# Gated mix of memory attention and a spectral filter: interleaved q/k scratch, gate weights by matmul, stores on GpSimd's queue

## The chip, the cores and the metric

The kernel runs on one core of one Trainium2 chip. The metric is the device time of one execution in microseconds. Three executions of the kernel before took 242.58, 243.16 and 244.0 us; their median is 243.16 us. A profile was taken of one further execution.

## The reference, cut to what matters

```python
def _A_ref(x, wq, wk, wv, wo, beta):        # S=2048, D=640, H=32 heads of 20, N=4 segments of L=512
    q, k, v = (heads(x @ w) for w in (wq, wk, wv))
    g = sigmoid(beta)
    for s in range(N):                       # per head: causal softmax inside the segment
        p = softmax(qs @ ks.T * Dh**-0.5 + mask)
        a_dot = p @ vs
        a_mem = (phi(qs) @ M) / (phi(qs) @ z + 1e-6)   # phi(t) = t+1 for t > 0, else exp(t)
        o = g * a_mem + (1 - g) * a_dot
        M, z = M + phi(ks).T @ vs, z + phi(ks).sum(rows)
    return o @ wo
def _B_ref(x, w_r, w_i):                     # spectral filter over the whole 2048 x 640
    return irfft2(rfft2(x) * (w_r + 1j * w_i))
gate = sigmoid((A_x * gate_w).sum(-1))       # one gate for each row
return gate * a + (1 - gate) * _B_ref(x)     # x is A_x
```

## The kernel before, in words

**Work.** One core does both branches. Branch A goes through four segments of 512 rows. For each segment the kernel transposes x, projects q and k in five tiles of 128 features (`proj_tile`), projects v (`v_tile`), and computes causal attention for eight groups of four heads: `qk_unit` multiplies q and k, ScalarE (ACT) takes the exponential into `ex` (line 1508), the upper triangle is set to zero by `mask` on GpSimd (POOL, affine select, lines 1540 and 1549) or on VectorE (DVE, a minimum with a table, lines 1539 and 1545), and `pv_flipped` or `pv_group` multiplies with v. The memory part reads the accumulated M with phi(q) (`mem_read`) and updates it with phi(k) (`mem_update`). Branch B is a two-dimensional Fourier transform as matmuls with tables: `fold`, then the stages F1, D, T, Tb, Db and Fb. `finish_tile` adds the last stage of B and the output projection of A in one PSUM bank, and stores the rows.

**Through DRAM and back.** Heads have 20 features, tiles of a projection 128. To bring the heads to partitions 0, 32, 64 and 96, each projected tile is stored to the DRAM tensor `qk_scr` (line 582, "qk_scr<-qu", in the first segment "qk_scr<-q") and loaded again into the padded tiles `qkp` ("qkp<-qk_scr", name `pad`, four loads for each half of a segment; `pad2` in the first half of the first segment). The scratch holds, for each segment and half, a block of 320 rows of q and a block of 320 rows of k; a row is 512 tokens, 1 KB. Tile 2 of the five lies across the halves, so it is stored by two DMAs of 64 rows each:

```python
if t == 2:
    for half, p0 in ((0, 0), (1, 64)):
        self.dma(... row(half, 256 - 256 * half), [L, 64], [1, L] ..., name="st_qk")
```

The numerators of attention go through `u_scr` in the same way ("u_scr<-ub", then "oU<-u_scr"), and the memory term of segments 1 and 2 through `o_scr` ("o_scr<-mem", name `st_o`, eight stores; loaded transposed as "mT<-o_scr", line 580).

**The gate.** The weights of the gate stand as a 641st column beside each of the five tiles of `wv`, so that the second half of the v projection (321 columns) gives the gate's logits as well. They are brought there by one DMA of 640 single elements (name `ld_gw`, "wv<-in_gate_w_dram").

**Queues and order.** All DMAs are issued on SyncE's queue (SP), but for one load at the start and eight quarter stores at the end on ACT's. POOL issues none. A queue works in order: an issue that waits for its data holds up every issue behind it. The order of all work is written out: `ORDER` lists operation numbers, each with the engine that takes it, and `Sched.schedule` goes through the list, places PSUM banks, and adds waits; `ENDED` gives a ranking by which several waits of one instruction are sorted. The times in `schedule` and in the table `QUEUE` serve this planner alone. Each instruction of an engine is issued in the list's order. All matmuls are issued at lines 546 and 548, copies from PSUM at 557 (ACT) and 559 (DVE), DMAs at 582, transposing DMAs at 580.

**Where output tiles go.** `finish_tile` fills one of four tiles `ot` in two halves and stores it with one DMA of 128 rows (name `st_out`, "out_dram<-ot", twelve of them, segments 0 to 2). The last segment stores quarters (`st_part`) from SP and ACT.

Of the kernel before, what the change touches and what calls it, by code (L numbers as in the profile page):

```python
# [9 lines left out]
BF = dt.bfloat16  # L10
F32 = dt.float32

P = 128
S = 2048
D = 640
H = 32
DH = 20
NSEG = 4
L = 512
# [25 lines left out]
class Op:  # L45
    __slots__ = ("id", "alts", "preds", "succs", "prio", "banks", "nbytes", "npred", "eng", "t0", "t1",
                 "stamp", "rank", "need_inc", "dyn", "first", "outside", "name", "dma", "key", "xfer", "lock", "mode", "emode", "hold", "width", "high", "follow")


class Sched:  # L50
# [9 lines left out]
    def op(self, alts, r=(), w=(), prio=0.0, nbytes=0, name="", after=(), dma=False, xfer=0.0, lock=False, mode=0, hold=False, width=16):  # L60
# [4 lines left out]
        o.high, o.follow = False, None  # L65
# [47 lines left out]
    def schedule(self, pools, order, ended, nsem=56):  # L113
# [42 lines left out]
        sems = [[0.0, i, None] for i in range(nsem)]  # L156
        issued = []
        self.order = []
# [49 lines left out]
        while len(self.order) < len(order):  # L208
# [19 lines left out]
            if e == "pe" and o.emode != mode:  # L228
                occ += self.COST[mode, o.emode]
                mode = o.emode  # L230
            free[e] = o.t1 = t + occ
            if e == "dve" and o.lock:
                port = t + occ
            if o.dma:
                if o.hold:
                    free[e] = max(free[e], max(ring) + 170.0)
                for q in range(o.width):
                    ring[q] = max(ring[q], free[e] + 1300.0) + o.xfer
# [6 lines left out]
                sems.sort(key=lambda q: (q[0], q[1]))  # L245
                sm = sems[0]
# [13 lines left out]
        self.nsem = nsem  # L260
# [208 lines left out]
def dap(ap, off, *dims):  # L469
    return bass.AP(tensor=ap.tensor, offset=ap.offset + off, ap=[list(q) for q in dims])  # L470
# [25 lines left out]
class Kern:  # L496
# [35 lines left out]
    def mms(self, items, r, w, prio, name="", extra=0.0, mode=0):  # L532
# [17 lines left out]
        op = self.Sc.op({"pe": (f, cost, 141.0)}, r=r, w=w, prio=prio, name=name, mode=mode)  # L550
        return op
# [24 lines left out]
    def dma(self, dst, src, nbytes, r, w, prio, tr=False, name="", after=(), queue="sp"):  # L576
        def f(e):
# [3 lines left out]
            with self.nc.allow_non_contiguous_dma(reason="small strided loads"):  # L581
                return e.dma_start(d_, s_)  # L582
        cost, work, width = self.QUEUE[name] if name in self.QUEUE else self.QUEUE[name, nbytes]
        queues = ("sp", "act") if name in self.EARLY else (queue,)
        return self.Sc.op({e: (f, cost, 0.0) for e in queues}, r=r, w=w, prio=prio, nbytes=nbytes, name=name, after=after,
                          dma=True, xfer=work, hold=tr and nbytes > 500000, width=width)

    EARLY = ("ld_wqa", "ld_wka", "ld_id")
    QUEUE = {
        "ld_W": (620.0, 450.0, 16), "dup_W": (480.0, 1900.0, 16), "ld_beta": (400.0, 120.0, 16), "ld_big": (500.0, 2900.0, 16), "ld_den": (520.0, 150.0, 16),  # L590
        "ld_fcat": (400.0, 350.0, 16), "ld_g": (400.0, 1500.0, 16), "ld_gc": (580.0, 200.0, 16), "ld_gw": (420.0, 600.0, 16),
        "ld_hm": (600.0, 850.0, 16), "ld_id": (400.0, 250.0, 16), "ld_x0": (450.0, 950.0, 16), "ld_tt": (530.0, 1650.0, 16), "ld_u": (500.0, 450.0, 16),
        "ld_wka": (520.0, 1100.0, 16), "ld_wkb": (450.0, 2200.0, 16), "ld_wqa": (500.0, 1100.0, 16), "ld_wqb": (500.0, 2200.0, 16),
        "ld_wo": (600.0, 700.0, 16), "ld_wo2": (600.0, 3000.0, 16), "ld_wv": (450.0, 3000.0, 16), "ld_x": (450.0, 950.0, 16),
        "oT": (1300.0, 750.0, 16), "pad2": (370.0, 350.0, 10), "pad": (400.0, 1250.0, 10), ("pkT", 131072): (1260.0, 600.0, 16), ("pkT", 262144): (1280.0, 1100.0, 16),
        ("st_qk", 65536): (450.0, 220.0, 16), ("st_qk", 131072): (480.0, 350.0, 16), ("st_qk", 262144): (480.0, 720.0, 16), "st_g": (430.0, 150.0, 4), "st_o": (660.0, 950.0, 8), "st_out": (560.0, 1900.0, 4),
        "st_part": (430.0, 250.0, 16), "st_u": (520.0, 700.0, 16), ("xT", 131072): (1240.0, 1300.0, 16), ("xT", 262144): (1700.0, 2300.0, 16),
        ("xT", 393216): (1400.0, 2600.0, 16), ("xT", 655360): (2950.0, 2100.0, 16)}
# [1276 lines left out]
```

## Time and profile before

| | |
|---|---|
| median of three executions | 243.16 us |
| the profiled execution | 242.17 us |
| its span, first to last instruction | 240.4 us |
| matmuls | 4361 |
| bytes moved by DMA | 43.46 MB in 58072 packets, 181 GB/s in the mean |
| DMAs issued by SP and by ACT | queues q1 (42.46 MB) and q10 (0.36 MB) |

The profile shows one execution. An engine's busy time is the time in which at least one of its instructions ran; PE is TensorE's matmuls and PEld its weight loads, which overlap. A row of the windows view gives, for one stretch of time, each engine's busy time and its number of instructions in brackets, then the clock granted to TensorE (1.00 is full), the busy share of the DMA engines, and GB/s. A row of the waits view says which engine and line waited, for what, and then the total in microseconds, the number of times, and the longest. A row of a tile's view gives the shortest, median and longest duration of one instruction in nanoseconds. The chain of waits goes back from the last instruction to what released it, step by step; "SPq" is SP issuing a DMA.

### The profile page before, as it was taken

Reading aid. Unit: us, or ns where it says so; the run is one execution under the profiler, and the core shown is the slowest. Engines: PE = TensorE matmul, PEld = TensorE weight load, DVE = VectorE, ACT = ScalarE, POOL = GpSimd, SP = SyncE. Lnnn points to the kernel's source line nnn. Section 1 sums busy time; section 2 is a strip of 40 time slices with the busy share of each in tenths; the row PEclk is TensorE's granted clock in tenths of the full one; section 3 lists DMA queues with packets and bytes.
Section 4 is the critical chain, followed back from the end, with each engine's and each line's share of the span. In section 5 each row is a group of like instructions: output and inputs, shape, how many; then the busy total and the mean of one; then the engine's idle time right before and its main releaser. Section 6 shows DMA issues by size and latency. Waiting matters only on the chain.

```text
span 240.4 us, 10161 instructions
## 1 busy us (share of the span) xinstructions
PE 228.9 (95%) x4361; PEld 146.3 (61%) x4361; DVE 203.8 (85%) x493; ACT 202.7 (84%) x253; POOL 92.9 (39%) x172
## 2 busy tenths in 40 slices
PE   7999799999999999999989999999999999999993
PEld 4666367666556674654656555565555667667883
DVE  0978888999999899999999999899999679747742
ACT  2398979999999999999999999899899977678630
POOL 5203415503655407250516733504546232272810
PEclk9999999999999999999999999999999999999999
DMA  7998988678979989849986748378759862782213
GB/s 195 373 182 264 198 270 176 148 239 211 213 146 241 221 215 226 200 136 154 216 246 162 229 129 223 92 197 201 197 154 223 209 151 79 105 90 92 77 43 108
DMA packets 58072, 43.46 MB, mean 181 GB/s; under 512 B 27628, under 2 KB 55724, under 8 KB 58028
## 3 DMA queue, kind: packets, MB, share of 16 engines
q1 hardware_dynamic: 57500, 42.46, 73.9%
q8 instruction: 34, 0.56, 1.0%
q10 hardware_dynamic: 528, 0.36, 0.5%
q14 instruction: 10, 0.08, 0.1%
HBM read 22.73 MB, written 12.20 MB: 145 GB/s over the span
## 4 chain that ended last, share of the span: by engine, by line
PE 60%; DVE 15%; ACT 12%; DMA 6%; SPq 3%; issue 3%; DVEq 0%
PE psum L548 53%; ACT ex L1508 9%; PE psum L546 7%; DMA hm<-tab_hmask 3%; DMA qk_scr<-qu 2%; SPq L582 2%; DMA u_scr<-ub 2%; DVE mem L1389 1%; DVE G L559 1%; DVE oU L1791 1%; DVE ub L559 1%; DVE ex L1545 1%; DVE Pt L1696 1%; ACT qu L557 1%; DVE dn L1381 1%
## 5 line engine op out<-in xcount | busy, mean ns | idle before, releaser
L1508 ACT ACTIVATE ex<-psum 128x2048 bf16<-128x2048 f32 (+4 forms) x92 | 138.6, 1507 | 12.2 <-PE psum L548 10.7
L1549 POOL TENSOR_SCALAR_AFFINE_SELECT ex<-ex 64x256 bf16<-64x256 bf16 x66 | 26.8, 427 | 64.3 <-ACT ex L1508 63.5
L1540 POOL TENSOR_SCALAR_AFFINE_SELECT ex<-ex 128x512 bf16<-128x512 bf16 x44 | 29.4, 678 | 31.7 <-DVE ex L1545 20.3
L548 PE MATMUL psum<-qkp 20*64 20x64 bf16 (+5 forms) x1024 | 31.4, 266 | 1.6 <-ACT ex L1508 0.9
L548 PE MATMUL psum<-wv,xT 128*64 128x320 bf16 (+3 forms) x240 | 26.6, 302 | 2.4 <-DMA wv<-in_A_wv_dram 1.5
L548 PE MATMUL psum<-xT,wk 128*128 128x256 bf16 (+1 forms) x280 | 28.3, 273 | 0.0
L548 PE MATMUL psum<-xT,wq 128*128 128x512 bf16 (+1 forms) x135 | 27.9, 380 | 0.0
L1696 DVE TENSOR_TENSOR Pt<-psum,Wt 128x644 bf16<-128x644 f32 x32 | 25.8, 820 | 1.4 <-PE psum L548 1.1
L548 PEld LDWEIGHTS psum<-xT,wk 128*128 128x128 bf16 (+1 forms) x280 | 20.9, 98 | 4.4 <-issue 0.4
L548 PEld LDWEIGHTS psum<-qkp 20*64 20x64 bf16 (+1 forms) x1024 | 12.1, 100 | 18.1 <-ACT ex L1508 10.9
L546 PE MATMUL psum<-wo,oU 128*32 128x320 bf16 x480 | 21.0, 299 | 0.0
L548 PEld LDWEIGHTS psum<-wv,xT 128*64 128x64 bf16 (+1 forms) x240 | 14.8, 105 | 9.4 <-DMA wv<-in_A_wv_dram 1.7
L559 DVE CAST ot<-psum 128x320 bf16<-128x320 f32 x20 | 9.4, 489 | 10.3 <-PE psum L546 4.5
L548 PE MATMUL psum<-ex,va 128*32 128x512 bf16 (+4 forms) x480 | 17.3, 274 | 0.1
L548 PE MATMUL psum<-big,Cp 128*128 128x321 bf16 (+1 forms) x96 | 16.7, 302 | 0.7 <-DVE rs L1587 0.3
L548 PE MATMUL psum<-tt,Pt 128*128 128x128 bf16 (+1 forms) x192 | 16.4, 221 | 0.0
L1298 ACT ACTIVATE et<-qu 128x512 bf16<-128x512 bf16 x25 | 15.6, 629 | 0.4 <-DVE phk L1311 0.4
L546 PEld LDWEIGHTS psum<-wo,oU 128*32 128x32 bf16 x480 | 12.8, 97 | 3.8 <-issue 0.6
L548 PE MATMUL psum<-big,Ac 128*32 128x160 bf16 (+2 forms) x384 | 14.4, 259 | 0.7 <-DVE mem L1385 0.5
L1545 DVE TENSOR_TENSOR ex<-ex,hm 128x512 bf16<-128x512 bf16 (+1 forms) x31 | 13.8, 453 | 1.3 <-ACT ex L1508 1.0
L548 PEld LDWEIGHTS psum<-tt,Pt 128*128 128x128 bf16 (+1 forms) x192 | 12.1, 102 | 4.4 <-issue 0.9
L548 PEld LDWEIGHTS psum<-xT,wq 128*128 128x128 bf16 (+1 forms) x135 | 9.2, 97 | 8.5 <-issue 1.8
(114 smaller groups left out, 420.6 us busy)
## 6 DMA issues: line engine op xcount, KB each, us to landing
qkp<-qk_scr SPq DMA_DIRECT2D x28, 160.0 KB
qk_scr<-qu SPq DMA_DIRECT2D x12, 256.0 KB, 3.6
tt<-tab_tt SPq DMA_DIRECT2D x8, 384.0 KB, 4.4
u_scr<-ub SPq DMA_DIRECT2D x12, 256.0 KB, 3.6
Wt<-Wt SPq DMA_DIRECT2D x8, 321.0 KB, 4.0
xsb<-in_A_x_dram SPq DMA_DIRECT2D x8, 320.0 KB, 5.4
oU<-u_scr SPq DMA_DIRECT2D x15, 128.0 KB, 3.2
out_dram<-ot SPq DMA_DIRECT2D x12, 160.0 KB
```

The source lines that it names most:

```text
L546: h = e.matmul(dst, wt, r_, start=st, stop=sp_, **{**kw, "tile_position": (0, q), "skip_group_check": True})
L548: h = e.matmul(o_, l_, r_, start=st, stop=sp_, **kw)
L557: alts["act"] = (lambda e: e.activation(dst(), src(), ACT.Copy), 65 + 0.833 * n, 110.0)
L559: alts["dve"] = (lambda e: e.tensor_copy(dst(), src()), 67 + 1.04 * n, 68.0)
L582: return e.dma_start(d_, s_)
L1298: self.one("act", lambda e: e.activation(et.ap(0, [1, L]), qsl(), ACT.Exp), L, [qb], [b("et", pi_)], late, fix=94, name="phi_exp")
L1381: self.one("dve", lambda e: e.reciprocal(dn.ap(32, [1, 32]), dn.ap(0, [1, 32])), 32, [b("dn", i % 2, q) for q in range(2)], [rb], prio, fi ...
L1508: self.one("act", lambda e, d=d, q=q: e.activation(self.ex.ap(*d), self.ps(bank, *q), ACT.Exp, scale=SC), n, [bank], [self.exb(s, 2 * pr + ...
L1540: pick = lambda e: e.affine_select(ex(), ex(), [[0, 4], [1, P]], ALU.is_ge, 0.0, base=0, channel_multiplier=-1)
L1545: least = lambda e: e.tensor_tensor(dst(), src(), self.hm.ap(880 + 64 * t, [0, 4], [0, 2], [1, 64], np_=nd), ALU.min)
L1549: h = e.affine_select(self.ex.ap(e0 + d, [1280, 4], [1, 64], p0=hp, np_=np_), self.ex.ap(e0 + q, [1280, 4], [1, 64], p0=hp, np_=np_), [[0, ...
L1696: self.one("dve", lambda e, x=x, Pt=Pt, Wt=Wt, wo_=wo_, bank=bank: e.tensor_tensor(Pt.ap(x * 644, [322, 2], [161, 2], [1, 161]), self.ps(b ...
```

## The change

- **Scratch.** `qk_scr` holds, for each segment and each of the 640 features, the row of q and behind it the row of k. A load into `qkp` finds q and k of a feature side by side and moves runs of 2 KB. In `qkp` the four blocks of q and the four of k alternate, and `qk_unit` and `proj_direct` address them so. The first half of the first segment (`pad2`) keeps runs of 1 KB.
- **Middle tile.** Tile 2 is stored by one DMA of 128 rows.
- **Gate weights.** They are loaded as five rows of 128 into the tile `dnc`, turned by a matmul with the identity (`gwT`, five columns), and copied from PSUM into the column of `wv` (`ev_gw`), after `wv` has been loaded.
- **Queues.** The stores `st_out` and `st_o` are issued on POOL's queue. Fifteen names (`SPARE`) may be issued by SP or POOL, as the order says.
- **Planner.** Costs of DMAs are set anew, a DMA on POOL has a semaphore of its own, the rule that ties neighbours on POOL (`follow`) now skips DMAs, and the planner counts PE's instructions in pieces of 256. None of this is an instruction on the chip by itself; it sets waits, banks and places.
- **Order.** `ORDER` and `ENDED` are new lists. By the new list POOL issues 39 DMAs: 12 `st_out`, 8 `st_o`, 7 `ld_W`, 3 `ld_g`, 2 `dup_W`, 2 `st_g`, and one each of `ld_x`, `ld_beta`, `ld_big`, `ld_tt`, `ld_den`. SP issues 192 in place of 241. POOL has 120 operations beside its DMAs in place of 135, DVE 498 in place of 493, ACT 274 in place of 261 with its DMAs (the loads `ld_wqa` and `ld_wka` are now among them).

```diff
-        for p, o in zip(queue["pool"], queue["pool"][1:]):
-            if p.high != o.high:
-                o.follow = p
+        own = [o for o in queue["pool"] if not o.dma]
+        for p, o in zip(own, own[1:]):
+            if p.high != o.high:
+                o.follow = p
...
+            if e == "pe":
+                c = 2.011 * o.count * (4 if o.mode < 0 and o.emode == 2 else 1)
+                while stream + c > 192 + 256 * len(pieces):
+                    x = t + occ * (192 + 256 * len(pieces) - stream) / c
+                    if pieces and x < pieces[-1]:
+                        occ += pieces[-1] - x
+                        x = pieces[-1]
+                    pieces.append(x + (3000.0, 2000.0, 1000.0)[min(len(pieces), 2)] + 2550.0)
+                stream += c
...
-        queues = ("sp", "act") if name in self.EARLY else (queue,)
+        queues = ("sp", "act") if name in self.EARLY else ("sp", "pool") if name in self.SPARE else ("pool",) if name in ("st_out", "st_o") else (queue,)
...
+    SPARE = ("ld_W", "dup_W", "ld_tt", "ld_gw", "ld_beta", "ld_hm", "ld_big", "ld_wv", "ld_x", "ld_wo", "ld_wo2", "ld_g", "ld_gc", "ld_den", "st_g")
...
-        self.qkd = nc.dram_tensor("qk_scr", (NSEG, 2, 2, 320, L), BF)
+        self.qkd = nc.dram_tensor("qk_scr", (NSEG, 640, 2, L), BF)
...
-        self.dma(lambda: self.wv.ap(D, [D + 1, 5], [1, 1]), lambda: dap(self.gw_d, 0, [1, P], [P, 5], [1, 1]),
-                 P * 5 * 64, [], [self.b("gw")], 0.31, name="ld_gw")
+        self.dma(lambda: self.dnc.ap(0, [1, P], np_=5), lambda: dap(self.gw_d, 0, [P, 5], [1, P]), 5 * 256, [], [self.b("dnc")], 0.31, name="ld_gw")
+        bank = Bank(1, "gen")
+        self.mms([(lambda: (self.ps(bank, 0, [1, 5]), self.dnc.ap(0, [1, P], np_=5), self.fcat.ap(P, [1, 5], np_=5), True, True, {"tile_position": (0, 0)}), 5)],
+                 [self.b("dnc"), self.b("id"), bank], [], 0.5, name="gwT", mode=1)
+        self.Sc.op(self.copy_alts(lambda: self.wv.ap(D, [D + 1, 5], [1, 1]), lambda: self.ps(bank, 0, [1, 5], [1, 1]), 5), r=[bank, self.b("wv")], w=[self.b("gw")], prio=0.5, name="ev_gw")
...
-                self.dma(lambda j=j, pad=pad: pad.ap(0, [L, 8], [1, L], p0=32 * j, np_=DH),
-                         lambda j=j, half=half: dap(self.qkd.ap(), ((2 * s + half) * 640 + 20 * j) * L, [L, DH], [80 * L, 8], [1, L]),
+                self.dma(lambda j=j, pad=pad: pad.ap(0, [2 * L, 4], [1, 2 * L], p0=32 * j, np_=DH),
+                         lambda j=j, half=half: dap(self.qkd.ap(), ((2 * s + half) * 640 + 40 * j) * L, [2 * L, DH], [160 * L, 4], [1, 2 * L]),
...
-            for half, p0 in ((0, 0), (1, 64)):
-                self.dma(lambda half=half, p0=p0: dap(self.qkd.ap(), row(half, 256 - 256 * half), [L, 64], [1, L]), lambda p0=p0: qt.ap(qo, [1, L], p0=p0, np_=64),
-                         64 * L * 2, both, [b(which + "d", s, half, 1 - half)], prio, name="st_qk")
+            self.dma(lambda: dap(self.qkd.ap(), row(256), [2 * L, P], [1, L]), lambda: qt.ap(qo, [1, L]),
+                     P * L * 2, [qb], [b(which + "d", s, half, 1 - half) for half in range(2)], prio, name="st_qk")
...
-            self.dma(lambda: dap(self.qkd.ap(), row(t // 4, (t - slot) * P - 320 * (t // 4)), [L, P], [P * L, n], [1, L]), lambda: qt.ap(o, [L, n], [1, L]),
+            self.dma(lambda: dap(self.qkd.ap(), row((t - slot) * P), [2 * L, P], [2 * P * L, n], [1, L]), lambda: qt.ap(o, [L, n], [1, L]),
...
-                        return (self.ps(bank, hh * 512 + o, [1, n], p0=p0, np_=m), pad.ap((4 + gl) * L + KPOS[j] + kc, [1, m], p0=32 * hh, np_=DH),
-                                pad.ap(gl * L + q0, *([[-64, 2], [1, 64]] if q0 + n > L else [[1, n]]), p0=32 * hh, np_=DH), True, True, {"tile_position": (32 * hh, p0)})
+                        return (self.ps(bank, hh * 512 + o, [1, n], p0=p0, np_=m), pad.ap((2 * gl + 1) * L + KPOS[j] + kc, [1, m], p0=32 * hh, np_=DH),
+                                pad.ap(2 * gl * L + q0, *([[-64, 2], [1, 64]] if q0 + n > L else [[1, n]]), p0=32 * hh, np_=DH), True, True, {"tile_position": (32 * hh, p0)})
```

More of the change, by code (lines that the diff above doesn't have):

```diff
@@ L46 @@
     __slots__ = ("id", "alts", "preds", "succs", "prio", "banks", "nbytes", "npred", "eng", "t0", "t1",
-                 "stamp", "rank", "need_inc", "dyn", "first", "outside", "name", "dma", "key", "xfer", "lock", "mode", "emode", "hold", "width", "high", "follow")
+                 "stamp", "rank", "need_inc", "dyn", "first", "outside", "name", "dma", "key", "xfer", "lock", "mode", "emode", "hold", "width", "high", "follow", "count")
 class Sched:
@@ L64, in op @@
         o = Op()
-        o.high, o.follow = False, None
+        o.high, o.follow, o.count = False, None, 0
         o.id = len(self.ops)
@@ L550, in mms @@
         op = self.Sc.op({"pe": (f, cost, 141.0)}, r=r, w=w, prio=prio, name=name, mode=mode)
+        op.count = len(items)
         return op
@@ L588 @@
+        return self.Sc.op({e: (f, max(cost, 600.0) + 50.0 if e == "pool" else cost, 300.0 + 900.0 * (e == "pool") + 700.0 * tr) for e in queues}, r=r, w=w, prio=prio, nbytes=nbytes, name=name, after=after,
+                          dma=True, xfer=work, hold=(tr and nbytes > 500000) + 2 * tr, width=width)
+    SPARE = ("ld_W", "dup_W", "ld_tt", "ld_gw", "ld_beta", "ld_hm", "ld_big", "ld_wv", "ld_x", "ld_wo", "ld_wo2", "ld_g", "ld_gc", "ld_den", "st_g")
     EARLY = ("ld_wqa", "ld_wka", "ld_id")
@@ L1182, in proj_direct @@
         b = self.b
-        w, p0_ = (self.wq, 0) if which == "q" else (self.wk, 4 * L)
+        w, p0_ = (self.wq, 0) if which == "q" else (self.wk, L)
         pad = self.qkp[0]
```

41 lines of the change are left out of this document (23 added, 18 removed), and 500 rows, old and new, of tables (ENDED, ORDER).

## The prediction

> **What bounds the kernel now.** The profiled execution took 242.17 us: a span of 240.4 and 1.77 around it. I read the page's busy time first, then the windows of 12 us, and then who waited for whom.
>
> ```profile
> PE 228.9 (95%) x4361; PEld 146.3 (61%) x4361; DVE 203.8 (85%) x493; ACT 202.7 (84%) x253; POOL 92.9 (39%) x172
> PE 60%; DVE 15%; ACT 12%; DMA 6%; SPq 3%; issue 3%; DVEq 0%
> ```
>
> PE is busy for all but 11.5 us, and 60% of the chain is PE. The change takes away no matmul, so those 11.5 us are nearly all there is to win. Where they lie:
>
> ```profile
> 0.00:12.00 12.00, 10.68 (x164) 6.51 (x164) 6.32 (x14) 3.73 (x6) 4.88 (x13) 1.00 0.89 283
> 24.00:36.00 12.00, 10.15 (x123) 6.17 (x122) 9.75 (x26) 10.16 (x22) 3.54 (x5) 1.00 0.94 233
> 60.00:72.00 12.00, 11.57 (x250) 6.57 (x243) 11.81 (x34) 11.85 (x15) 7.30 (x18) 1.00 0.93 181
> 120.00:132.00 12.00, 11.19 (x232) 7.08 (x224) 11.87 (x29) 11.43 (x11) 4.87 (x10) 1.00 0.77 205
> 144.00:156.00 12.00, 11.37 (x205) 6.75 (x195) 10.67 (x22) 10.70 (x13) 5.09 (x11) 1.00 0.57 158
> 168.00:180.00 12.00, 11.06 (x188) 6.30 (x189) 11.86 (x30) 10.87 (x14) 5.91 (x11) 1.00 0.62 172
> 192.00:204.00 12.00, 11.29 (x307) 8.14 (x307) 10.61 (x29) 8.98 (x11) 3.12 (x6) 1.00 0.58 119
> 216.00:228.00 12.00, 12.00 (x393) 9.46 (x384) 9.49 (x23) 9.04 (x13) 7.00 (x12) 1.00 0.26 81
> 228.00:240.00 12.00, 8.83 (x244) 7.75 (x240) 4.62 (x11) 2.48 (x5) 0.80 (x1) 1.00 0.27 79
> ```
>
> The first numbers after the comma are PE, PEld, DVE, ACT and POOL; the last three are clock, DMA share and GB/s. PE stands idle 1.3 us before its first operand and 3.2 in the last stretch, after its last matmuls, which the change leaves as they are. One gap of 1.85 lies in 24 to 36; five more, of 0.4 to 0.9 each, make 3.3 between 60 and 204. So some 5 us in the middle are open to the change. In 60 to 72 DVE and ACT are as full as PE; POOL alone has room. The clock is full, so nothing is lost there.
>
> ```profile
> PE psum L548 <- DMA wv<-in_A_wv_dram: 1.5, 1, 1.5
> PE psum L548 <- DVE qu L559: 0.6, 1, 0.6
> DVE qu L559 <- DMA qk_scr<-qu: 0.9, 1, 0.9
> DVE ot L559 <- DMA out_dram<-ot: 2.0, 2, 1.1
> PEld psum L548 <- issue: 15.5, 67, 0.7
> PEld psum L548 <- POOL ex L1540: 0.9, 3, 0.4
> ```
>
> Each row is the total, the times and the longest wait. Only two of PE's waits lead to a DMA: for wv at 28 us, and for a projection buffer that its store still held at 152. The small waits are for evacuations, and these the order sets.
>
> **Part 1: gate weights.**
>
> ```profile
> 8.82 0.38 SPq L582 DMA_DIRECT2D wv<-in_gate_w_dram  x1
> 9.24 6.38 SPq L580 DMA_TRANSPOSE xT<-in_A_x_dram  x1
> 22.23 0.50 SPq L582 DMA_DIRECT2D wv<-in_A_wv_dram  x1
> wv<-in_gate_w_dram SPq DMA_DIRECT2D x1, 1.2 KB, 6.8
> wv<-in_A_wv_dram SPq DMA_DIRECT2D x1, 800.0 KB, 7.1
> ```
>
> The old load brings 640 elements one by one; it lands 6.8 us after its issue, for 1.2 KB. The new one brings five rows. It is still one SP issue, so what can be saved is time on the DMA engines, not on SP. But wv is issued at 22.23, long after the gate weights landed at 15.6, because SP was held by the transposes of x until 15.62 and then waited for a projection tile. So the gate load isn't what makes wv late. What may help is that the new order puts fewer of the eight x loads ahead of wv (one goes to GpSimd, one behind). Bounds: a gain of 1.5 (all of PE's wait) and a loss of 0.5 (two stores and a transpose of keys stand ahead of wv now). I take a gain of 0.4.
>
> ```profile
> L548 PE MATMUL psum<-fcat,omh 128*8 128x128 bf16 x8 | 1.1, 219 | 0.0
> L1340 ACT ACTIVATE gate<-psum 128x1 f32<-128x1 f32 x8 | 1.3, 165 | 0.1
> ```
>
> Added: a matmul of 5 columns and a copy of 5 columns. The nearest rows are a 219 ns matmul and a 165 ns one-column activation. The copy waits for wv and for the matmul, and the second value tile waits for the copy; behind it on ACT stand the first value evacuations. Cost 0.2, between 0 and 0.6 (if copy and hand-over all stand on PE's path).
>
> **Part 2: interleaved scratch, one store for the middle tile.**
>
> ```profile
> L582 SPq DMA_DIRECT2D qk_scr<-qu x24: 372/506/1021, 34.7 to 176.3; - x24
> L582 SPq DMA_DIRECT2D qkp<-qk_scr x36: 273/406/1148, 28.4 to 194.4; - x36
> qk_scr<-qu SPq DMA_DIRECT2D x12, 64.0 KB
> qk_scr<-q SPq DMA_DIRECT2D x4, 64.0 KB, 5.4
> 145.40 0.37 SPq L582
> 145.94 0.52 SPq L582
> 146.51 0.69 SPq L582
> 147.24 5.50 DMA qk_scr<-qu
> 152.83 0.70 DVE qu L559
> ```
>
> Sixteen half stores become eight: 8 x 0.506 = 4.0 us less of issuing on SP. The 28 large loads into qkp keep their issues, but their runs double from 1 KB to 2 KB. No row above has PE waiting for qkp by a DMA, so I give the longer runs nothing; what hides them is that these loads go out well ahead of their stage. If that cover were gone, a load would cost PE the 4.0 us median to landing. Where SP does count is the last five rows, from the chain: at 145.4 a store of u, a table copy and a store of the memory term go out ahead of the store of q or k, which takes 5.50, and the evacuation waits for its buffer. One of these four leaves SP, another may be half of a pair. PE's wait there was 0.6. With the smaller ones of its kind at 115 (a store of u) I take a gain of 0.7; bounds 0 and 1.7, about half of the 3.3 between 60 and 204.
>
> **Part 3: stores on GpSimd's queue.**
>
> ```profile
> L582 SPq DMA_DIRECT2D o_scr<-mem x8: 587/688/1337, 77.4 to 148.3; - x8
> L582 SPq DMA_DIRECT2D out_dram<-ot x20: 314/544/1255, 195.0 to 238.2; - x20
> SPq L582 <- DVE ot L559: 9.4, 2, 6.7
> POOL ex L1549 <- ACT ex L1508: 63.5, 16, 10.4
> POOL ex L1540 <- DVE ex L1545: 20.3, 7, 8.7
> 1.29 2.46 POOL L1100 MEMSET va<- 128x2832 bf16 x1
> ```
>
> SP loses 8 x 0.688 + 12 x 0.544 = 12.0 us of issues, and the wait of 9.4 in which it stood before a finished output tile while loads queued behind it. GpSimd gains 20 issues, and by the order list 19 loads that may go by either queue (tables, masks of the FFT, gates). No row shows a DMA issued by GpSimd. Below, it costs what SP pays, 0.54; above, as long as GpSimd's longest single instruction, 2.46. I take 1.0, since most of its rows lie under 1: 39 us, beside 147 idle. Each store waits for its tile (DVE, ACT), and behind it stand the causal masks of ex, for which PV on PE waits. Of POOL's idle time 63.5 + 20.3 us in 23 gaps, 3.6 each, is before just these masks, so a store of 1 us that is put into such a gap is hidden. The list also gives 15 of POOL's small operations to DVE (12 of them masks of about 0.5 us), and DVE gives about as much time in evacuations to ACT. Loss 0.3, bounds 0 and 5 (see the rivals). For SP's freedom late in the kernel: DVE waited 2.0 for output tiles, and 192 to 204 lost 0.7. Gain 0.4, bounds 0 and 0.7.
>
> [...]
>
> **Part 4: own order.** All queues are written anew. PE has the same sequence of stages; the first loads of wq and wk go from SP to ACT, which in 0 to 12 is busy for 3.7 us only, so they cost nothing there. What it can win is the rest of the 5 us in the middle, and part of PEld's 15.5 us of "issue". After 0.4, 0.7 and 0.4 some 3.5 remain; I give the order a quarter to a third of it, 0.9; bounds -3.5 and +2, since a new order opens gaps of its own (a gap here is 0.3 to 0.9, and three or four more would be 2).
>
> **Sum.** -0.4 + 0.2 - 0.7 + 0.3 - 0.4 - 0.9 = -1.9 on 242.17, so 240.3 for an execution like the profiled one. The median shown is 0.99 above it: 243.16 - 1.9 = 241.3.
>
> **The rivals.** *Most of the gaps close.* All of the 5 us in the middle less 0.5 for the new work: 243.16 - 4.5 = 238.7, and 237 if PEld's "issue" shrinks too. For it: SP is on the chain, and is relieved of 16 us of issues. Against: most of PE's small waits are for evacuations on DVE and ACT, which get no lighter.
>
> *Nothing moves.* SP waits elsewhere, wv lands when it did, and order and added work cancel: 243.2. For it: only 1.5 + 0.6 us of PE's waits name a DMA.
>
> *Slower: GpSimd's queue takes SP's place.* A store stands at its head until DVE and ACT have filled the tile, and the masks behind it come late. It decides where a store with its issue outlasts the gap of 3.6. If one store in four of the 20 finds no gap, 5 issues of 1.0 reach PE, as PE has no slack; with 2.46 each it is 12.3. So 241.3 + 5 = 246.3, up to 253.6. In its favour: the rows of 60 to 72 show DVE at 11.81, with no room for masks that are taken from GpSimd. Against it: PEld waited only 0.9 for the masks of line 1540. [...]
>
> **How the numbers follow.** Forecast (239.8 to 242.4) 0.42; most gaps close 0.20; nothing moves 0.13; slower 0.25. The measurement tells 0.5%, 1.2 us, from no change: faster is below 241.9, slower above 244.4. The forecast's upper edge falls in "same": 0.04 of it goes there. So faster 0.58, same 0.17, slower 0.25. For 8 in 10 the range is 237.4 to 246.5: it holds the close of most gaps and the slower rival up to one store in four; the likeliest case alone has 239.8 to 242.4.
>
> **What would show it.** Right: no 640-element load; PE's idle in 24 to 36 falls below 1.85 by about 0.4; SP's rows have 8 + 20 issues fewer of these kinds; PE busy stays at 229 in a shorter span; masks on POOL keep gaps ahead of them. Wrong: PE or PEld waits for "POOL ex", or POOL's DMA issues of 2 us and more (the slower rival); PE's gaps unchanged in number with other names (nothing moves). A PE busy time that falls by more than 1 us would mean that stalls inside "busy" went away, which my sum does not count.

## The result, and the profile after

The changed kernel took 257.94 us in the median of four executions (255.71 to 264.36), the kernel before 243.58 beside it. The ratio is 1.0521, with a 95% interval of 1.0445 to 1.0596: slower by 5.2%. The prediction said 241.3, with 246.5 as its upper end. Ratios here are taken from those executions of each kernel that lie within some 1.5% of its fastest, so a median over all executions can say more than its ratio (`a_old_order_o_pool`); here two of the four are such, as are two of `a_old_order`'s four and one of `b_new_order`'s, which so has no ratio.

The profiled execution took 256.11 us, its span 254.4. In the code after, the lines have moved: matmuls stand at 563 and 565 (546 and 548 before), copies from PSUM at 575 and 577 (557 and 559), DMAs at 600 (582), the exponential at 1529 (1508); in some runs the later ones lie a few lines further down. From the page after: busy time, the clock in 40 slices, the chain.

```profile
PE 234.8 (92%) x4350; PEld 148.7 (58%) x4362; DVE 200.7 (79%) x498; ACT 206.0 (81%) x264; POOL 107.1 (42%) x186
PEclk9869999999999999999999999999999985997999
PE 57%; ACT 21%; DVE 10%; DMA 7%; issue 2%; POOL 1%; ACTq 0%
PE psum L565 52%; ACT ex L1529 16%; PE psum L563 5%; DMA wq<-in_A_wq_dram 4%; DMA out_dram<-ot 3%; DVE qu L577 1%; DVE Pt L1717 1%; ACT va L575 1%; DVE oU L1812 1%; DVE ub L577 1%; DVE Ac L577 1%; ACT G L575 1%; ACT gate L1361 1%; ACT qu L575 1%; ACT et L1319 1%
```

The span grew by 14.0 us. PE's idle time went from 11.5 to 19.6 (254.4 less 234.8), which is 8.1; its busy time grew by 5.9 with one matmul more (a dozen records are missing from this trace, so a little of the idle time may be theirs). This busy time grows without work, and with it the granted clock falls: the second line is no longer 9 throughout, but lower at the start and at five sixths of the span. The windows, in the columns of the prediction's:

```profile
0.00:12.00 12.00, 6.29 (x34) 2.81 (x34) 3.75 (x10) 2.86 (x4) 5.07 (x13) 0.94 0.77 247
24.00:36.00 12.00, 11.89 (x94) 6.63 (x95) 11.11 (x29) 11.01 (x18) 1.53 (x3) 1.00 0.92 251
60.00:72.00 12.00, 11.83 (x244) 7.18 (x244) 11.82 (x32) 11.80 (x22) 4.62 (x11) 1.00 0.79 163
120.00:132.00 12.00, 10.74 (x246) 6.86 (x235) 11.30 (x31) 11.62 (x13) 5.14 (x12) 1.00 0.65 156
192.00:204.00 12.00, 10.79 (x277) 6.61 (x275) 10.11 (x24) 10.15 (x15) 5.79 (x11) 1.00 0.73 163
204.00:216.00 12.00, 11.24 (x238) 7.52 (x231) 7.05 (x21) 7.25 (x9) 7.73 (x9) 0.72 0.46 115
216.00:228.00 12.00, 12.00 (x360) 8.18 (x356) 5.64 (x12) 9.31 (x10) 5.71 (x10) 1.00 0.72 94
228.00:240.00 12.00, 10.28 (x284) 7.61 (x276) 8.89 (x23) 6.06 (x7) 6.36 (x9) 0.86 0.15 30
```

The first window holds 6.29 us of PE for 10.68 before, and 34 matmuls for 164. In 24 to 36, where I expected a small gain, PE is full: wv no longer holds it. In 60 to 72 half a gap is closed; 120 to 132 and 192 to 204 have 1.3 and 1.2 us of idle time, for 0.8 and 0.7 before. The stretch from 204 on, where PE was full before, now has gaps and a clock of 0.72 and 0.86. Who waited for whom, in the waits view of the kernel after:

```profile
PE psum L565 <- DMA wq<-in_A_wq_dram: 4.2, 1, 4.2
PE psum L565 <- ACT ex L1529: 3.4, 14, 0.3
PE psum L565 <- DVE ot L577: 1.7, 1, 1.7
DVE ot L577 <- DMA out_dram<-ot: 2.5, 1, 2.5
```

Three sorts of PE's waits are new or larger: for the first weights, for the exponential (14 small waits; before 4, of 0.9 together), and for an output tile that its store still held. The chain at the start (start, length, what), and the windows of 2 us behind two of PE's gaps:

```profile
0.81 0.50 ACTq L600
...
1.34 0.56 ACTq L600
...
1.93 10.24 DMA wq<-in_A_wq_dram
...
12.21 13.53 PE psum L565 x170
```

```profile
10.00:12.00 2.00, 0.00 (x0) 0.00 (x0) 1.86 (x6) 0.00 (x0) 0.00 (x0) 0.64 0.94 343
12.00:14.00 2.00, 1.79 (x24) 0.97 (x24) 1.08 (x4) 0.00 (x0) 0.77 (x1) 0.50 0.48 91
14.00:16.00 2.00, 2.00 (x23) 0.77 (x24) 1.30 (x4) 0.60 (x1) 0.00 (x0) 0.50 1.02 368
206.00:208.00 2.00, 1.30 (x33) 0.94 (x29) 1.75 (x7) 1.09 (x2) 1.27 (x2) 1.00 0.26 20
208.00:210.00 2.00, 1.94 (x28) 1.21 (x28) 1.38 (x5) 1.40 (x1) 1.98 (x4) 0.64 0.41 98
210.00:212.00 2.00, 2.00 (x61) 1.56 (x57) 0.32 (x3) 1.14 (x3) 2.00 (x3) 0.50 0.42 109
212.00:214.00 2.00, 2.00 (x40) 1.13 (x36) 1.22 (x4) 1.72 (x2) 0.73 (x1) 0.50 0.09 38
```

The load of wq, now third on ACT's queue, takes 10.24 us to land. PE's gap of 4.2 ends at 12.2, and the clock is 0.50 until 17. The gap before 208 is 0.7 us, and again 0.50 follows, to 215. The start times of the exponentials place the loss: the first stands 8.1 us later than before, the tenth 5.6, number 69 of 92 7.2, number 89 14.0. So some 8 us were lost at the start, of which 2.5 came back soon; 1.6 were lost in the middle, and nearly 7 behind number 69, from 193 us on.

### The profile page after: what moved, and what is told of

Read it like the earlier page. It is cut to its first block, busy times and chain, and to the rows that moved or that the text cites. A ratio compares the mean times of both kernels' runs of the same rounds, so it can differ in the third digit from the quotient of the medians.

```text
span 254.4 us, 10120 instructions
## 1 busy us (share of the span) xinstructions
PE 234.8 (92%) x4350; PEld 148.7 (58%) x4362; DVE 200.7 (79%) x498; ACT 206.0 (81%) x264; POOL 107.1 (42%) x186
## 4 chain that ended last, share of the span: by engine, by line
PE 57%; ACT 21%; DVE 10%; DMA 7%; issue 2%; POOL 1%; ACTq 0%
PE psum L565 52%; ACT ex L1529 16%; PE psum L563 5%; DMA wq<-in_A_wq_dram 4%; DMA out_dram<-ot 3%; DVE qu L577 1%; DVE Pt L1717 1%; ACT va L575 1%; DVE oU L1812 1%; DVE ub L577 1%; DVE Ac L577 1%; ACT G L575 1%; ACT gate L1361 1%; ACT qu L575 1%; ACT et L1319 1%
## 5 line engine op out<-in xcount | busy, mean ns | idle before, releaser
L1561 POOL TENSOR_SCALAR_AFFINE_SELECT ex<-ex 128x512 bf16<-128x512 bf16 x42 | 28.7, 692 | 49.0 <-DVE ex L1566 41.2
L565 PE MATMUL psum<-xT,wq 128*128 128x512 bf16 (+1 forms) x123 | 26.0, 449 | 5.2 <-DMA wq<-in_A_wq_dram 4.2
L1570 POOL TENSOR_SCALAR_AFFINE_SELECT ex<-ex 64x256 bf16<-64x256 bf16 x46 | 19.0, 439 | 27.6 <-ACT ex L1529 27.4
L565 PE MATMUL psum<-xT,wk 128*128 128x256 bf16 (+1 forms) x280 | 29.0, 282 | 0.1
L565 PEld LDWEIGHTS psum<-qkp 20*64 20x64 bf16 (+1 forms) x1024 | 12.2, 101 | 21.0 <-ACT ex L1529 12.7
L563 PE MATMUL psum<-wo,oU 128*32 128x320 bf16 x480 | 22.6, 317 | 1.0 <-DVE oU L1812 1.0
L577 DVE CAST ot<-psum 128x320 bf16<-128x320 f32 x18 | 8.5, 488 | 14.7 <-PE psum L563 8.2
L565 PEld LDWEIGHTS psum<-wv,xT 128*64 128x64 bf16 (+1 forms) x240 | 15.2, 105 | 6.6 <-issue 1.1
L1566 DVE TENSOR_TENSOR ex<-ex,hm 128x512 bf16<-128x512 bf16 (+1 forms) x41 | 17.4, 435 | 1.9 <-ACT ex L1529 1.8
L565 PE MATMUL psum<-ex,va 128*32 128x512 bf16 (+4 forms) x480 | 17.4, 275 | 0.1
L565 PE MATMUL psum<-big,Cp 128*128 128x321 bf16 (+1 forms) x96 | 17.4, 312 | 0.0
L563 PEld LDWEIGHTS psum<-wo,oU 128*32 128x32 bf16 x480 | 13.6, 102 | 6.1 <-DVE oU L1812 1.3
L565 PE MATMUL psum<-big,Ac 128*32 128x322 bf16 (+2 forms) x384 | 14.1, 259 | 0.3 <-DVE ub L577 0.2
```

The lines of the kernel that those rows point to most:

```text
L563: h = e.matmul(dst, wt, r_, start=st, stop=sp_, **{**kw, "tile_position": (0, q), "skip_group_check": True})
L565: h = e.matmul(o_, l_, r_, start=st, stop=sp_, **kw)
L577: alts["dve"] = (lambda e: e.tensor_copy(dst(), src()), 67 + 1.04 * n, 68.0)
L1561: pick = lambda e: e.affine_select(ex(), ex(), [[0, 4], [1, P]], ALU.is_ge, 0.0, base=0, channel_multiplier=-1)
L1566: least = lambda e: e.tensor_tensor(dst(), src(), self.hm.ap(880 + 64 * t, [0, 4], [0, 2], [1, 64], np_=nd), ALU.min)
L1570: h = e.affine_select(self.ex.ap(e0 + d, [1280, 4], [1, 64], p0=hp, np_=np_), self.ex.ap(e0 + q, [1280, 4], [1, 64], p0=hp, np_=np_), [[0, ...
```

## The experiments

My first theory (S and T) was that the start (weights late, half clock) and the last stage (output stores on GpSimd) hold the loss. The rival (O) was that the new order itself does. "Changed" and "before" name the two kernels' code; an order is the list `ORDER`.

**First four: undo start and output stores.**

`a_weights_on_sp`: the changed kernel with the two loads on SP behind the first x loads. The list holds numbers; here it is shortened and has names.

```diff
-    ORDER: ld_wka act, ld_id act, ld_wqa act, ... ld_x0, ld_x0 sp
+    ORDER: ld_id act, ... ld_x0, ld_x0, ld_wqa, ld_wka sp
```

> The changed kernel with one edit: the first loads of wq and wk are issued by SP again, behind the two loads of x's first rows, as in the kernel before. Theory S+T (the start: on ACT's queue these loads share the DMA engines with what SP issues and land late, and TensorE's clock then falls; the tail: output tiles are held by their stores on GpSimd's queue): the start's share goes, about 5.5 us, so about 250.5, with the first exponential near 12 us in place of 19.9 and a granted clock of 1.00 from 8 to 24 us. Rival O (the new order as a whole is slower, not these two places): stays at 256. Rival G (GpSimd's DMA issues hold up the masks all along): 256 less at most 2.

Measured: 254.21 us, ratio 1.0467 (1.0395 to 1.0540). In the profiled execution the granted clock was 1.0 throughout (0.985 to 0.993 in the mean of the other three), and the first exponential stood 1.8 us late for 8.1. Yet by the ratios only 0.5 points, 1.3 us, came back where I expected 5.5, and the intervals don't tell that from nothing. PE's idle time was now 21.8 us, more than in the changed kernel: of the 6.3 us gained at the first exponential 2.8 were left at the tenth and 1.1 at number 69.

`a_out_on_sp`: output stores on SP.

```diff
- else ("pool",) if name in ("st_out", "st_o") else (queue,)
+ else ("pool",) if name == "st_o" else (queue,)
```

> The changed kernel with one edit: the twelve output stores of segments 0 to 2 are issued by SP, at their places in the new order; the memory-term stores stay with GpSimd. Theory S+T: the tail's share goes, 6 to 8 us, so 248 to 250; no wait of DVE for an output tile of 2.5 us, and the clock stays at 1.00 after 205. Rival O: stays at 256, since the tail's slip at 207 begins before a store is waited for. Rival G: 253, as only 12 of the 39 issues leave GpSimd.

Measured: 254.02, ratio 1.0422 (1.0350 to 1.0494). By the ratios 1.0 point came back, 2.4 us for the 6 to 8 that I expected.

`a_weights_and_out_on_sp`: both edits.

> The changed kernel with both edits: wq and wk on SP at the start, output stores on SP. Theory S+T: both shares go, 242 to 245, about the kernel before. Rival O: over 250. Rival G: about 251.

Measured: 254.46, ratio 1.0390 (1.0310 to 1.0469). S and T together explain a quarter of the loss, 1.3 of 5.2 points; the theory falls as an account of the whole.

`b_weights_on_act`: the kernel before, with these loads on ACT as in the changed one.

> The kernel before with one edit: the first loads of wk and wq are issued by ACT at the start (wk, identity, wq), as in the changed kernel; all else as before. Theory S+T: the start's share appears alone, 5 to 6 us, so about 248.5, with the first matmul on wq at 11 to 12 us in place of 7.1 and the granted clock below 1.00 for some us. Rivals O and G: 243, since neither the order nor GpSimd has changed.

Measured: 246.19, ratio 1.0126 (1.0066 to 1.0185). This edit alone costs some 3 us. Here PE's gap at the start was not wq's. From the waits view:

```profile
PE psum L548 <- DMA fcat<-tab_fcat: 1.9, 1, 1.9
PE psum L548 <- DMA xT<-in_A_x_dram: 1.5, 1, 1.5
```

The first row is the table with the identity, which before stood alone on ACT's queue and now has the load of wk ahead of it: PE began to transpose the first x tile at 6.38 us for 4.28. The second row lies at 68 us; that it comes of the start is not shown.

**Second four: order against parts.** The changed code was given the order of before (each merged store at the place of its first half, `gwT` and `ev_gw` ahead of the first v projection), and the code before the new order, with all its loads and stores on SP.

`a_old_order`: the changed code in the old order; loads on SP, output and memory-term stores on GpSimd.

> The changed kernel's code (q and k scratch interleaved by row, one store of a middle tile, gate weights turned on TensorE, output and memory-term stores on GpSimd's queue) in the order of the kernel before: first projection weights on SP, all loads on SP, each merged store at the place of the first of the two that it replaces, the gate-weight matmul ahead of the first v projection. Theory N (the new order itself opens the PE gaps, about 10 us of them, most of them small and many in the last stage): 242 to 246 us, within 1% of the kernel before. Rival P (the parts cost it: scratch layout, gate weights, stores on GpSimd): 250 us or more.

Measured: 251.46, ratio 1.0417 (1.0304 to 1.0529).

`a_old_order_stores_sp`: the same with these stores on SP.

> As the run above, and the output and memory-term stores back on SP: left are the scratch interleaved by row, the merged store and the gate weights turned on TensorE. Theory N: 242 to 245, and at most 2 us from the run above either way. Rival P: if the stores on GpSimd are the part that costs, below 246 while the run above is at 250 or more; if layout or gate weights cost, 250 or more here too.

Measured: 241.65, ratio 0.9992 (0.9950 to 1.0034).

`b_new_order`: the code before in the new order, first weights on ACT.

> The kernel before's code (its scratch layout, its split stores, its gate weights, all stores and loads on SP) in the order of the changed kernel, with the first projection weights on ACT as that order has them. Theory N: 254 to 258 us, the whole loss of the changed kernel from the order alone. Rival P: 245 to 248, the kernel before and some 3 us for the late weights at the start.

Measured: 251.34, between what the theories gave. But the four executions go from 247.26, in rival P's range, to 253.55, nearly theory N's, so this run decides little.

`b_new_order_weights_sp`: the same with these weights on SP.

> As the run above with the first projection weights back on SP behind the first two x loads, the identity ahead of them. Theory N: 250 to 255 us (what the changed kernel showed with the same edit was 254.2). Rival P: 242 to 246.

Measured: 249.1, ratio 1.0284 (1.0172 to 1.0396).

Both N and P hold in part, which neither allowed for: scratch, merged store and gate weights cost nothing that can be measured; the stores on GpSimd cost some 10 us in the old order; the new order costs without any of them. What is harmless can be seen in `a_old_order_stores_sp`, by its page and one window:

```profile
PE 228.4 (96%) x4362; PEld 145.3 (61%) x4362; DVE 201.8 (85%) x493; ACT 202.6 (85%) x254; POOL 93.3 (39%) x172
```

```profile
24.00:36.00 12.00, 11.88 (x136) 7.21 (x134) 10.67 (x29) 11.60 (x27) 4.46 (x6) 1.00 0.94 271
```

PE's gap of 1.85 in 24 to 36 is gone.

**Third four: which transfers.**

`a_old_order_out_pool`: the old order, output stores alone on GpSimd.

> The changed kernel's code in the order of the kernel before, with the output stores alone on GpSimd's queue and the memory-term stores on SP (with both on GpSimd 251.5 us, with both on SP 241.7). Theory G (an output issue holds GpSimd some 0.70 us, and in the last stage, where it makes the masks, adds the memory term and scales, its queue is then full): 248 to 252, nearly all of the loss. Rival M (the memory-term stores hold it): 241 to 243.

Measured: 248.94, ratio 1.0244 (1.0168 to 1.0320).

`a_old_order_o_pool`: memory-term stores alone on GpSimd.

> The same with the memory-term stores alone on GpSimd's queue and the output stores on SP. Theory G: 241 to 244, since these eight stores are issued ahead of the last stage. Rival M: 248 to 252.

Measured: 244.68, ratio 0.9964 (0.9911 to 1.0016): no loss that can be told. Theory G's forecast holds: alone, the memory-term stores cost nothing and the twelve output stores 2.4%. Both together cost 4.2% (`a_old_order`), so 1.7 points, just clear of the noise, come only when both are there; why, no run shows. The last stage in one window, all output stores on SP and then on GpSimd:

```profile
200.00:236.00 36.00, 34.66 (x1027) 26.43 (x1024) 22.94 (x52) 21.31 (x27) 13.85 (x22) 1.00 0.45 85
```

```profile
200.00:236.00 36.00, 34.01 (x908) 23.56 (x901) 22.49 (x54) 21.59 (x25) 20.85 (x32) 0.88 0.42 78
```

The fifth busy time is POOL's: 7.0 us more, ten instructions more. PE has nearly the same busy time, but 908 matmuls for 1027: the clock is 0.88. Between the two executions PE's busy time differs by 3.4 us (231.8 and 228.4) and its idle time by 5.0 (15.2 and 10.2). In POOL's timeline of the kernel with the stores on GpSimd (start, length, what):

```profile
228.33 0.70 POOL L600 DMA_DIRECT2D out_dram<-ot  x1
229.05 0.79 POOL L1579 TENSOR_SCALAR_AFFINE_SELECT ex<-ex 64x256 bf16<-64x256 bf16 x2
229.78 0.82 POOL L1570 TENSOR_SCALAR_AFFINE_SELECT ex<-ex 128x512 bf16<-128x512 bf16 x1
230.56 0.70 POOL L600 DMA_DIRECT2D out_dram<-ot  x1
231.30 1.70 POOL L1280 TENSOR_SCALAR fbn<-fbg 128x512 bf16<-128x512 bf16 x1
```

Each row starts where the one before ends: the queue is full, stores ahead of masks and of the scaling `fbn`. Its waits, and the clock behind:

```profile
PE psum L565 <- POOL ex L1579: 0.9, 1, 0.9
PE psum L565 <- POOL fbn L1280: 0.8, 1, 0.8
DVE ot L577 <- DMA out_dram<-ot: 3.6, 2, 2.1
```

```profile
232.00:234.00 2.00, 1.16 (x24) 0.77 (x25) 1.84 (x5) 0.60 (x1) 1.76 (x2) 0.85 0.28 39
234.00:236.00 2.00, 2.00 (x33) 1.08 (x23) 0.00 (x0) 0.00 (x0) 0.00 (x0) 0.50 0.17 62
```

`a_stores_on_sp`: the changed kernel, first weights and both kinds of store on SP; its 19 loads and small stores stay on GpSimd.

> The changed kernel with the first weights, the output stores and the memory-term stores on SP; left on GpSimd's queue are its 19 loads and small stores, and the order is the new one. With the memory-term stores still on GpSimd it was 254.5, and the new order in the kernel before's code, all on SP, took 249.1: about 5 us lie between. If the memory-term stores hold these 5 us: 248 to 250. If the loads on GpSimd do: 253 to 255.

Measured: 251.8, ratio 1.0366 (1.0271 to 1.0460).

`a_all_on_sp`: these loads on SP as well.

> The same with the loads and small stores on SP too: of the change only the order, the scratch layout, the merged store and the gate weights are left. Theory Q (queues hold the 5 us that the order does not): 248 to 250. Rival D (layout, merged store or gate weights cost in this order, though not in the old one): 253 to 255.

Measured: 247.25, ratio 1.0148 (1.0001 to 1.0295). So Q, not D: the loads on GpSimd cost some 4.5 us in the new order, though the two intervals overlap at their ends. What stays is the order. Page and waits of this kernel:

```profile
PE 227.3 (93%) x4350; PEld 146.1 (60%) x4362; DVE 202.3 (83%) x498; ACT 206.3 (84%) x264; POOL 81.5 (33%) x147
```

```profile
PE psum L565 <- ACT ex L1535: 3.5, 14, 0.4
```

Its span is 244.9 at a full clock, so the order's loss is idle time of PE: 17.6 us for 10.2 in the old order (with a dozen records missing again; in `b_new_order_weights_sp`, where none are, 245.4 less 228.4, 17.0). ACT does 3.7 us more and POOL 11.8 less than with the old order; PE waits 3.5 us for exponentials in place of 0.9.

**Fourth four: where in the order, and what of a store.**

`h_new_then_old` and `h_old_then_new`: everything on SP, the two orders joined at the same set of finished instructions. The edit in short; the kernels hold the joined lists written out.

```diff
+ORDER = [v for v in NEW if v in FRONT] + OLD[cut:]
+ORDER = OLD[:cut] + [v for v in NEW if v not in FRONT]
```

> All loads and stores on SP, the changed kernel's layout and gate weights; the instructions ahead of exp 56 of 80 in the new order, the rest in the order of the kernel before. All old took 241.7 us, all new 247.3. Theory S (the new order loses in small pieces all along, since its score matmuls stand right behind the exp that frees their bank: 3.5 us of such waits against 0.9): 244 to 246, since at that exp the new order was 4.4 us later. Rival L (the loss is made in the last stage): 241 to 243.

> The same the other way round: the old order up to exp 56 of 80, then the new one. Theory S: 242 to 244. Rival L: 245 to 248.

Measured: 249.99, ratio 1.0259 (1.0179 to 1.0338), and 244.0, ratio 1.0071 (1.0035 to 1.0107). The front of the new order holds most of the loss, so L falls and S is right in direction. The first hybrid lies above S's range, and its interval overlaps that of the whole new order (1.0001 to 1.0295), so the split can't be given in microseconds. In its trace exponential 53, ahead of the seam, started at 159.9 us (at 154.2 in the old order, at 157.8 with the new one throughout); behind the seam PE stood for 2.1 us at 187, and the clock was 0.50 from 190 to 197.

`a_old_order_out_pool_ot7`: output stores on GpSimd, old order, 7 output tiles. One more line, not shown, takes the eighth x tile out of what the evacuation `ev_Tb` must follow.

```diff
-self.ot = [TL(f"ot{i}", [P, D]) for i in range(4)]      k4 = self.finc % 4
+self.ot = [TL(f"ot{i}", [P, D]) for i in range(7)]      k4 = self.finc % 7
```

> The changed kernel's code in the old order with the output stores alone on GpSimd (248.9 us), with 7 output tiles in SBUF for 4. Theory B (an output store lands 4.8 us after its issue on GpSimd against 1.8 on SP, which holds the four output tiles, and with them the evictions and the PSUM banks): 242 to 245. Rival W (what costs is GpSimd's own time, 0.70 us for each issue ahead of masks and scalings): 247.5 to 250.

Measured: 247.69, ratio 1.0150 (1.0064 to 1.0235).

`a_old_order_out_pool_adds_dve`: 4 tiles; six additions moved from POOL to DVE.

> The same kernel with 4 output tiles and the six additions of the memory term that GpSimd did (0.8 us each, most of them in the last stage) on DVE at the same places of the order. Theory W: 243 to 246, since some 5 us of GpSimd's time come free where it holds masks. Theory B: 247.5 to 250.

Measured: 249.38, ratio 1.0213 (1.0126 to 1.0299).

B's premise was misread: the 1.8 us are those of the quarter stores of 40 KB, and no view gives the landing of the stores of 160 KB on SP. With 7 tiles DVE's wait of 3.6 for output stores is gone, and the ratio is lower by 0.9 points, inside the two intervals. Moving the additions brings nothing that can be told, but this does not refute W. In both traces a store of 0.70 us still stands straight ahead of the last masks and of `fbn`; PE waits for these two for 0.8 and 0.8 us with 7 tiles, for 0.9 and 1.1 with the additions on DVE, and the clock then falls to 0.50.

**Last two: place in GpSimd's queue.**

`a_old_order_out_pool_late`: 7 tiles, each output store three places down in GpSimd's queue.

> The kernel with the output stores on GpSimd, the old order and 7 output tiles (247.7 us), with each output store moved three places down in GpSimd's queue, behind three masks, additions or scalings of its own: the same instructions, queue and transfers. Theory W2 (a store's 0.70 us, and its wait for its eviction, stand ahead of masks and scalings that PE waits for, and the clock then falls to half for some us after each such gap): 242 to 245. Rival R (GpSimd's whole load in the last stage, or the transfers, not the place): 246.5 to 249.

Measured: 251.97, ratio 1.0314 (1.0192 to 1.0436). Later stores didn't help, as R says. It is no clean test of W2: in the trace, of the longest of the four executions, another store (at 235.29) now stands straight ahead of the mask at 236.00, for which PE still waits 0.8 us.

`a_stores_on_sp_scale_dve`: loads on GpSimd, new order; two multiplications moved to DVE. What they were to remove, in the trace of `a_stores_on_sp`:

```profile
POOL oU L1818 <- DMA oU<-u_scr: 3.7, 1, 3.7
PE psum L565 <- POOL ex L1576: 1.9, 1, 1.9
```

```profile
186.00:188.00 2.00, 0.12 (x1) 0.03 (x1) 0.49 (x1) 1.79 (x2) 2.00 (x4) 1.00 0.84 241
190.00:192.00 2.00, 2.00 (x9) 1.12 (x8) 1.05 (x3) 1.92 (x2) 1.56 (x1) 0.50 0.59 181
```

> The changed kernel with first weights and all stores on SP, loads on GpSimd (251.8 us, and 247.3 with the loads on SP too), with the two multiplications of a q-memory row by its denominators that GpSimd does on DVE. In its trace the first waited 3.7 us for its load with four masks behind it, PE waited 1.9 us for the last of them, and the granted clock was then 0.5 for 3 us. Theory M (this one queue of waiting holds most of what the loads on GpSimd cost): 247.5 to 250. Rival K (the loads cost in many places): 250.5 to 253.

Measured: 251.75, ratio 1.0381 (1.0292 to 1.0470): no gain. The wait at 186 was gone, but PE now waited elsewhere, and its clock fell there:

```profile
PE psum L565 <- DVE Ac L577: 2.5, 1, 2.5
```

```profile
62.00:64.00 2.00, 0.23 (x8) 0.20 (x12) 1.51 (x4) 1.33 (x1) 0.63 (x1) 1.00 0.17 36
64.00:66.00 2.00, 2.00 (x48) 1.38 (x44) 1.55 (x5) 0.00 (x0) 0.49 (x2) 0.60 0.71 150
```

M falls, and K's range holds. That with the loads on GpSimd the new order has many places that are late by little, and that taking one away shows the next, fits this, but rests on one removed wait.

## Why the prediction was wrong

**Parts 1 and 2 cost nothing, but the wait for wv went in another way than I said.** Gate weights, interleaved scratch and merged store were to bring 0.9 us in sum; alone, in the old order, they gave a ratio of 0.9992 (0.9950 to 1.0034), which neither confirms nor refutes 0.4%. No loss hides in these parts. PE's wait for wv was gone there and in the changed kernel. I had put this down to fewer x loads ahead of wv in the new order. But it went in the old order too, where wv was issued at 22.18 us for 22.23, and PE began with it at 28.2 for 29.4; and in the new order with all transfers on SP PE waited 0.5 for it again. So here the row that I named as a sign came true by luck; why wv landed sooner is open. One sum was off by little: the five gaps between 60 and 204 make 3.5 us, not 3.3.

**Part 3 failed on the output stores.** The price of an issue was right: 0.69 to 0.80 us, inside my bounds of 0.54 and 2.46 and under the 1.0 that I took.

```profile
L600 POOL DMA_DIRECT2D out_dram<-ot x12: 688/706/802, 205.0 to 242.2; - x12
L600 POOL DMA_DIRECT2D o_scr<-mem x8: 598/628/710, 80.2 to 159.9; - x8
```

What failed is the step that hid these issues in gaps of 3.6 us. That mean was taken over the whole kernel. The eight memory-term stores lie in the middle, where such gaps are, and cost nothing that can be measured. The twelve output stores all lie behind 190 us, where POOL goes from 13.85 to 20.85 us of 36: in the old order they cost 2.5% where I had -0.1 us for the part. The slower rival named this mechanism, and in `a_old_order_out_pool` its rows are there, PE waiting for "POOL ex" and for `fbn`. In the changed kernel they are not: none of PE's waits names POOL, and no issue was longer than 0.80 us, so both of the rival's signs failed; what PE waited for there is an output tile, the row "DVE ot" of 1.7. Its price of 5 us, from five issues of 1.0 that reach PE, comes near the 6.1 that 2.5% are, but by another count: of 8.4 us between the two spans, 3.4 are PE running longer at a lower clock; so the nearness is luck. Its 246.3 was too low since order, loads and start came on top. In `a_old_order_out_pool` no issue was longer than 0.89 us either. What exactly of a store costs stays open: more tiles, less work on POOL and a later place each left most of it, but also left a store straight ahead of a mask that PE waits for.

**The loads on GpSimd had no price of their own.** I counted them into the 39 us of issues and called these hidden. With the new order they cost 2.2 points, the largest step there by the middle values. The 39 us are issuing alone. In `a_stores_on_sp` six of the 19 loads stood at the head of GpSimd's queue for 22.8 us in sum, until a buffer or an earlier transfer was ready, and all behind them stood too. The two longest:

```profile
POOL Wt L600 <- DVE phk L1337: 8.5, 1, 8.5
POOL tt L600 <- PE psum L565: 5.5, 1, 5.5
```

That this is what costs is not shown: one of PE's waits there names POOL, of 1.9, and taking that away brought no gain.

**Part 4 failed twice.** First, "they cost nothing there": I asked whether ACT had time to issue, and not when the weights land.

```profile
wq<-in_A_wq_dram ACTq DMA_DIRECT2D x1, 240.0 KB, 10.2
```

```profile
wq<-in_A_wq_dram SPq DMA_DIRECT2D x1, 240.0 KB, 5.2
```

The first row is the changed kernel's, the second that of the changed code in the old order. Both loads were issued at nearly the same time, at 1.93 and 1.82 us. On SP it stood third, behind two x tiles; on ACT it stood behind wk and the identity, while SP issued beta and two more x tiles beside it, and it landed 5 us later. Whether the place or the company did this, no run separates. The identity came late too, at 6.15 us (3.37 in `a_weights_on_sp`), and the first transposing waited for it; the x tile itself was not late (4.13 and 4.17). Alone this start costs 1.3% in the old order.

Second, the order was to gain 0.9, at most lose 2. With all transfers on SP it lost 1.5% (0.01 to 2.95) in the changed code and 2.8% (1.7 to 4.0) in the code before, 3.6 to 6.9 us of 243. I priced it by the gaps there were to close, and gave gaps that a new list opens only "three or four more". PE had some 17 us of idle time in place of 10.2, with the 14 waits for exponentials as the largest regular item, 2.6 us more. That the evacuations moved from DVE to ACT cause these waits is likely by ACT's 3.7 us more, but no run shows it.

**"The clock is full, so nothing is lost there" failed.** A full clock was a property of that schedule, not a constant. Of the 14.0 us, 5.9 are busy time, and in kernels at full clock this time stayed within 227.3 and 230.8; so at least 4 of them are the clock, which stood at 0.50 for 17.1 us in all (10.6 to 17.4, 208.5 to 215.4, 232.4 to 235.9).

The costs don't add up. In the old order 1.3% for the start and 4.2% for the stores (2.5% for the output's alone); in the new one the steps are 1.5 for the order, 2.2 for the loads, 0.2 for the memory-term stores, 0.8 for the output stores and 0.5 for the first weights, each uncertain by a point or more. That a wait which comes late hides the next one would explain this, but is not shown.

No kernel beat the one before: `a_old_order_o_pool` with 0.9964 and `a_old_order_stores_sp` with 0.9992 can't be told from it.

## What to carry to other kernels

Where one engine is 95% busy, a new order of all work is a risk before it is a gain: price it by the waits it can open, and test it apart from the edits that came with it. A store moved to a second queue must be set beside the load of that engine in the store's own stage, not in the mean over the kernel. For a load moved to another issuer, ask when it lands beside the other transfers, not whether the issuer is free. And a short gap can cost the clock as well: in the changed kernel one of 0.7 us was followed by 0.50 for 6.83 us.

## What the runs showed of the hardware

The clock was more easily lost than I had thought. In the changed kernel a gap of 0.7 us at 207 was followed by 0.50 for 6.83 us, and with the one of 4.2 at the start the clock was 0.50 for as long; in `a_weights_on_sp` gaps of 2.0 us at 36 and 1.5 at 211 were followed by none, and the clock was 1.0 throughout. So the length of one gap does not decide. What goes with the fall can be counted in the traces of the kernel before and of the changed one. In the latter the three spells at 0.50 last 6.83, 6.83 and 3.41 us, and the full clock between them 191.14 and 17.07, all whole multiples of 3.41. Cut both traces into stretches of this length, from the first clock record (6.12 and 7.16 us) to 5 us before the end of the span. For each stretch, add up the columns that the matmuls begun in it send through the array, each weighted by the share of 128 x 128 that its weights fill: "128*32 128x320" counts 320 x 32/128 = 80. Of 132 stretches at full clock three were followed by 0.50, those with the lowest sums: 1280 at 7.2 us, 2667 at 205.1, which has the gap of 0.7, and 3080 at 229.0. The lowest sum that the full clock outlasted is 3296, in the kernel before at 26.6, where PE waited 1.5 us for wv. Of the five stretches at 0.50, those with 2048 and 2790 were followed by 0.50 again, those with 3744, 4096 and 4160 by the full clock. Without the weights the sums don't part the two: 12616 columns in the stretch at 229.0, 5184 in the one at 26.6.

This is a count over two traces; no run changed this sum alone, and why the clock falls is not shown.
